# Fused linear attention and squared-ReLU MLP: where the attention's squares are kept, and how its slices are dealt out to the strips

## The chip, the cores and the metric

The kernel runs on one core of a Trainium2 chip. The metric is the device time of one execution in microseconds, from launch to end on that core. Lower is better. All arithmetic is fp32.

## The reference

Attention without a softmax feeds a two-layer MLP. `q`, `k` and `v` have 8 batches, 8 heads, 576 positions and a head size of 64.

```python
kv  = einsum('bhsd,bhse->bhde', k, v)          # 64 x 64 per head
out = einsum('bhsd,bhde->bhse', q, kv)
rms = sqrt(mean(out * out, axis=-1) + 1e-06)   # per head and position
x   = (out / rms * g_norm)                     # (8, 8, 576, 64)
x   = x.transpose(0, 2, 1, 3).reshape(4608, 512)
h   = x @ w_in                                 # 512 x 2048
r   = maximum(h, 0.0)
y   = (r * r) @ w_out                          # 2048 x 512
```

## The kernel before

The 4608 tokens are cut into 9 strips of 512, each of 4 tiles of 128 tokens. A strip has an up part (x times w_in, ReLU, square) and a down part (times w_out). The matrix products are Strassen-like: strip 0 is plain in its up part, strip 1 has one level there, and strips from 2 on (`DEEP_UP = 2`) have two levels. From strip 2 on the up part is 55 slots (`up_slot`), in each of which one or a few small products run as groups of four or eight 128 x 128 matmuls into a PSUM bank; the partial products that later sums need are copied out of PSUM as snapshots. In the profile these are the matmuls of L1109, the sums of L1121 on VectorE (DVE) or GpSimd (POOL), and the copies `snap` of L1126 on ScalarE (ACT). The ReLU and the square are L1059 and L1060. The down part is 14 steps of L921 matmuls, whose results are gathered in tiles `o_sb` and stored.

The attention that a strip needs is worked out while the strips before it run. It is one long list of steps, `slices`, and a step is a Python function that issues the instructions of one small piece of work:

- `transposed_query` (T) makes the transposed queries qT of a batch and a pair of heads,
- `key_value` (K) multiplies k and v to kv (L395) and copies it out (L398, L399),
- `query` multiplies qT and kv into PSUM, `x_ps` (L427), for up to two tiles of tokens, and squares the result on ACT (`sq`, L436); with extra arguments it also issues the `key_value` of a later batch,
- `mean_roots` reduces the squares on DVE (`ms`, L444) and takes the root,
- `normalized` divides (`x_n`, DVE, L495),
- `squares_x` transposes blocks of x_n on DVE into `x_q`, `send_x` stores x_q to DRAM (`x_d`, L571), and `fetch_x` reads it back transposed (`xT`, L577).

For strips 0 and 1 the shorter forms `query_means`, `roots_normalized` and `features` are used, in which the transposition is done by TensorE. `ready[s]` is the number of slices that have to be issued before strip s starts. Between the slots of strip s the function `attend` issues slices until the number due by then is reached, dealt out evenly. From strip 2 on:

```python
goal, begun = ready.get(s + 1, len(slices)), slice_at[0]
...
attend(begun + (goal - begun) * min(i + 1, 37) // 37)
```

So the order of the instructions on each engine is the order in which the Python functions are called; nothing reorders it afterwards. Each engine runs its instructions in that order and waits at an instruction whose inputs or whose output buffer aren't there yet. Nearly all DMAs are issued on SyncE's queue (SP), which waits in the same way. Each DMA also uses one of eight semaphores in turn, and so waits for the one eight before it.

Buffers come from pools that hand their buffers out in turn. Those that matter here are `xn` (3 buffers: x_n, x_q, and the squares sq), `c` (6 buffers: the snapshots and o_sb), `qkv` (2 each of q, k and v), and `stream` (4 buffers `w_blk`, the blocks of weights that are read from DRAM for each strip, issued by `stream`). The loads of q, k and v are issued by `load_next`, and in part one by one between the slots (`drip`; those of q are queued up by `drip_queries`). The remainder of 64 positions per batch is loaded by itself (`q_rest`, `k_rest`, `v_rest`).

Of the kernel before, what the change touches and what calls it, by code (L numbers as in the profile page):

```python
# [10 lines left out]
FP32 = mybir.dt.float32  # L11
# [9 lines left out]
def kernel(  # L21
# [47 lines left out]
    NT = 4  # L69
# [4 lines left out]
    DEEP_UP = 2  # L74
# [9 lines left out]
    xn_pool = ctx.enter_context(tc.tile_pool(name="xn", bufs=3))  # L84
# [86 lines left out]
    units = [(b, p) for b in range(B) for p in range(NP)]  # L171
    to_load = iter(units)

    owed = deque()

    def load_next(q_eng=nc.sync, names="kvq"):
        u = next(to_load, None)
        if u is not None:
            load(*u, q_eng, names)
            owed.extend([u] if "q" not in names else [])  # L180

    drips, rest_drips = deque(), deque()

# [4 lines left out]
                return f(*a)  # L188

    def drip_queries():  # L190
        if owed:
            u = owed.popleft()
            drips.extend((load, (*u, nc.sync, "q", (2 * h, 2 * h + 1))) for h in range(2))


# [216 lines left out]
    def products_x(ns):  # L412

        ps = apsum.tile([P, 2, 2, d_model // 2], FP32, name="x_ps", tag="x", bufs=1)
        for p in range(NP):
            for i, n in enumerate(ns):
                m, c = divmod(n, PAIR)
                for h in range(2):
                    half = slice(REST * h, REST * (h + 1))
                    if c == C:  # L420
                        q, b = qT["rest", m, p], 2 * m + h
                    else:
                        b, c_b = (2 * m, c) if c < C else (2 * m + 1, c - C - 1)
                        q = qT[b, p][:, c_b]
                    for r in range(2):
                        row = slice(D * r, D * (r + 1))
                        nc.tensor.matmul(  # L427
                            ps[half, r, i, ts(p, D)], lhsT=q[row, half], rhs=kvd[b, p][row, row], start=True, stop=True
                        )
        return ps  # L430

    def squared_parts(parts):
        sqs = []
        for ps in parts:
            sqs.append(xn_pool.tile(list(ps.shape), FP32, name="sq", tag="x_n"))
            nc.scalar.activation(sqs[-1], ps, AF.Square)  # L436
        return sqs

    def mean_of(sqs):
        ms = small.tile([P, 2, H], FP32, name="ms", tag="ms")[:, : len(sqs)]  # L440
        for i, sq in enumerate(sqs):
            if len(sq.shape) == 3:
                sq = sq.rearrange("p r e -> p (r e)")
            nc.vector.reduce_sum(out=ms[:, i], in_=by_head(sq), axis=AX.X)  # L444
        nc.vector.tensor_scalar(out=ms, in0=ms, scalar1=1.0 / D, scalar2=EPS, op0=ALU.mult, op1=ALU.add)
        return ms
# [17 lines left out]
    def query(ns, *keys):  # L464
        ps = products_x(ns)
        if keys:
            key_value(*keys)
        parts = [ps[:, :, i] for i in range(len(ns))]
        queried.append((parts, squared_parts(parts)))

    def query_means(ns):
        query(ns)
        parts, sqs = queried.pop()
        queried.append((parts, mean_of(sqs)))

    def roots_normalized(ns):
        parts, ms = queried.pop()
# [151 lines left out]
        slices += [(features, (n,)) for n in pair]  # L629
    ready[1] = len(slices)  # L630
    T, K, last = transposed_query, key_value, query_pairs(1)[2]
    slices += [(K, (2, 0, 1)), (T, (2, 0)), (query_means, (last,)), (T, (2, 1)), (roots_normalized, (last,))]
    slices += [(K, (2, 2, 3)), (features, (last[0],))]
    for b in range(2, B):
        fetch(1)
        slices += [(T, (b, p)) for p in (2, 3)]
        for pair in query_pairs(b):
            ahead = b + 1 < B and pair == query_pairs(b)[-1]
            slices.append((query, (pair, *((b + 1, 0, 1) if ahead else ()))))
            if ahead:  # L640
                slices += [(T, (b + 1, p)) for p in (0, 1)]
            slices.append((mean_roots, (pair,)))
            fetch(1)
            slices.append((normalized, (pair,)))
            fetch(1)
            slices += [(squares_x, (n,)) for n in pair]
            slices += [(send_x, (n,)) for n in pair]
            fetches.extend(pair)
            if ahead:
                fetch(1)  # L650
                slices.append((K, (b + 1, 2, 3)))
# [3 lines left out]
    def attend(n):  # L655
        while slice_at[0] < min(n, len(slices)):
            fn, a = slices[slice_at[0]]
            fn(*a)
            slice_at[0] += 1
# [499 lines left out]
    for s in range(N_STRIP):  # L1159
        attend(ready[s])  # L1160
        if s == DEEP_UP - 1:
            while queried:
                attend(slice_at[0] + 1)
            psums.close()
            fpsum = ctx.enter_context(tc.tile_pool(name="fpsum", bufs=5, space=bass.MemoryType.PSUM, reuse_waits="tile"))
            apsum = ctx.enter_context(tc.tile_pool(name="apsum", bufs=1, space=bass.MemoryType.PSUM, reuse_waits="tile"))
        if s >= DEEP_UP:
            steps = [(0.5, up_slot, (s, slot)) for slot in range(55)]
        elif s == 0:
            steps = [(2, up_first, (g, fh, i)) for g in range(NG) for fh in range(2) for i in range(2)]  # L1170
        else:
            steps = [(1, up, (s, g, p)) for g in range(NG) for p in ORDER]
        n_up = len(steps)
        if s < DEEP:

            steps += [(2, down, (s, p, i)) for p in (ORDER if s else (1, 2, 5, 6, 7, 3, 4)) for i in range(2)]
        else:
            steps += [(2, down_deep, (s, k, i)) for k in range(7) for i in range(2)]
        goal, begun = ready.get(s + 1, len(slices)), slice_at[0]
        total, done = sum(w for w, _, _ in steps), 0  # L1180
        for i, (w, fn, a) in enumerate(steps):
            if s == 0 and i < n_up:

                if 4 <= i < 11:
                    convert(5 + (3 * i + 2) // 4)
                if i in (4, 6, 8):
                    load_next()
                if i == 5:
                    load_rest(1, nc.sync)
                if i == 12:  # L1190
                    for b in range(2):
                        load_q_rest(b, nc.sync)
            elif s == 0 and i == n_up:
                convert(len(conversions))
                conv.close()

                stream_pool = ctx.enter_context(tc.tile_pool(name="stream", bufs=4, reuse_waits="tile"))
                sum_pool = ctx.enter_context(tc.tile_pool(name="sum", bufs=8, reuse_waits="tile"))
            if s == 0 and n_up <= i < n_up + 2:
                for g in range(2 * (i - n_up), 2 * (i - n_up) + 2):  # L1200
                    sum_g1(0, g)
            if s == 0 and n_up + 2 <= i < n_up + 4:
                for g in range(2 * (i - n_up) - 4, 2 * (i - n_up) - 2):
                    sum_g3(0, g)
            fn(*a)
            if s == 0 and i < 4:

                convert((3, 4, 5, 7)[i])
            done += w
            if s:  # L1210
                if i < n_up or i % 2:
                    drip(s == DEEP or i % 2 == 1)
                if s >= DEEP_UP:
                    attend(begun + (goal - begun) * min(i + 1, 37) // 37)
                else:
                    attend(begun + (goal - begun) * min(i + 1, n_up) // n_up)
                if s == DEEP and i == n_up - 3:
                    leaf_sums(s, 4)
                if s == 1 and i in range(3, 24, 3):
                    deep_sums_in((1, 6, 5, 4, 0, 2, 3)[i // 3 - 1])  # L1220
                if s == 1 and i in (n_up - 4, n_up - 2):
                    stream(2)
                continue
            if i == n_up + 1:
                stream()
            if i == n_up + 11:
                load_next()
            if i == n_up + 9:
                load_rest(2, nc.sync)
                load_q_rest(2, nc.sync)  # L1230
            if i - n_up in (7, 8, 9, 12):
                sums_in((7, 8, 9, 12).index(i - n_up))
            if i == n_up + 11:
                sums_x(1)
            n = i + 1 - (n_up - 6)
            pairs, m = divmod(max(n - 2 * NP, 0), 3)
            attend(min(ready[0] + min(max(n, 0), 2 * NP) + (n >= 2 * NP) + 4 * pairs + (0, 2, 2)[m], goal))
            if 11 <= i < n_up:

                convert(5 + (3 * i + 2) // 4)  # L1240
# [30 lines left out]
```

## Time and profile before

| | |
|---|---|
| median of 3 runs | 938.55 us (934.13 to 942.07) |
| profiled execution, whole | 936.43 us |
| its span in the profile | 934.6 us |
| mean granted TensorE clock | 0.983 |
| TensorE busy, matmuls / weight loads | 95% / 89% |
| DVE, ACT, POOL busy | 79%, 34%, 33% |
| DMA | 235.74 MB, mean 252 GB/s |
| chain that ended last | PE 74%, DVE 11%, DMA 9% |

The span is the time between the first and the last instruction of one execution under the profiler; 1.8 us of the execution lie outside it. PE is TensorE's matmuls and PEld its weight loads. A row of a timeline gives start, busy time, engine, line, operation, the tiles out and in, and in brackets the time that the engine was idle before it, with what released it. In a table of windows the columns after the window are its length, the busy time of each engine with the number of instructions, the granted clock as a share of full speed, the busy share of the DMA engines, and GB/s.

### The profile page before, as it was taken

Reading aid. Unit: us, or ns where it says so; the run is one execution under the profiler, and the core shown is the slowest. Engines: PE = TensorE matmul, PEld = TensorE weight load, DVE = VectorE, ACT = ScalarE, POOL = GpSimd, SP = SyncE. Lnnn points to the kernel's source line nnn. Section 1 sums busy time; section 2 is a strip of 40 time slices with the busy share of each in tenths; the row PEclk is TensorE's granted clock in tenths of the full one; section 3 lists DMA queues with packets and bytes.
Section 4 is the critical chain, followed back from the end, with each engine's and each line's share of the span. In section 5 each row is a group of like instructions: output and inputs, shape, how many; then the busy total and the mean of one; then the engine's idle time right before and its main releaser. Section 6 shows DMA issues by size and latency. Waiting matters only on the chain.

```text
span 934.6 us, 20804 instructions
## 1 busy us (share of the span) xinstructions
PE 890.0 (95%) x8246; PEld 830.9 (89%) x8246; DVE 738.8 (79%) x1258; ACT 318.2 (34%) x638; POOL 305.1 (33%) x315
## 2 busy tenths in 40 slices
PE   7999997999999999899998999699999999999998
PEld 6434786888989999899998999699999999999998
DVE  3899968778867996689777877589689967985886
ACT  4797350330024601280127112360155016302710
POOL 0000002810247505460455044330464147234700
PEclk7999999999999999999999999899999999999999
DMA  9699998879898786878776887878756866685385
GB/s 279 216 285 315 271 349 273 226 225 364 300 229 254 235 319 216 226 223 316 254 198 197 290 299 229 222 251 313 241 166 230 308 220 197 256 300 175 139 298 188
DMA packets 173810, 235.74 MB, mean 252 GB/s; under 512 B 85008, under 2 KB 138768, under 8 KB 165264
## 3 DMA queue, kind: packets, MB, share of 16 engines
q1 hardware_dynamic: 173392, 234.27, 77.8%
q8 instruction: 65, 1.06, 0.5%
q14 instruction: 33, 0.27, 0.1%
q10 hardware_dynamic: 320, 0.13, 0.1%
HBM read 197.66 MB, written 36.70 MB: 251 GB/s over the span
## 4 chain that ended last, share of the span: by engine, by line
PE 74%; DVE 11%; DMA 9%; issue 2%; SPq 2%; ACT 1%; DVEq 0%; ACTq 0%
PE ps_B L921 20%; PE ps_A L1109 17%; PE ps_A L921 15%; PE ps_B L1109 8%; PE ps_C L1109 4%; PE ps_A L700 3%; DMA x_d<-x_q 2%; PE x_ps L427 2%; PE kv_ps L395 1%; DVE w_c L251 1%; PE ps_B L700 1%; DMA w_blk<-w_in_deep 1%; DMA w_out<-w_in 1%; PE ps_C L700 1%; DMA k_rest<-in_k_dram 1%
## 5 line engine op out<-in xcount | busy, mean ns | idle before, releaser
L921 PE MATMUL ps_B<-w_blk,g_s 128*128 128x128 f32 x1024 | 125.9, 275 | 0.0
L921 PEld LDWEIGHTS ps_B<-w_blk,g_s 128*128 128x128 f32 x1024 | 120.1, 192 | 0.0
L1109 PE MATMUL ps_A<-x_l,w_in 128*128 128x128 f32 x784 | 107.0, 280 | 8.7 <-ACT snap L1126 5.8
L1109 PEld LDWEIGHTS ps_A<-x_l,w_in 128*128 128x128 f32 x784 | 97.6, 196 | 10.1 <-ACT snap L1126 5.3
L921 PE MATMUL ps_B<-w_blk,gt 128*128 128x128 f32 x768 | 97.6, 275 | 1.7 <-DMA w_blk<-w_out 1.3
L271 POOL TENSOR_TENSOR x_l<-xT 128x256 f32<-128x256 f32 x21 | 15.4, 735 | 248.9 <-PE ps_A L921 187.8
L921 PEld LDWEIGHTS ps_B<-w_blk,gt 128*128 128x128 f32 x768 | 91.4, 192 | 2.4 <-PE ps_A L700 1.3
L921 PE MATMUL ps_A<-w_blk,g_s 128*128 128x128 f32 x768 | 93.6, 275 | 0.0
L1121 POOL TENSOR_TENSOR snap<-snap,gt 128x512 f32<-128x512 f32 x35 | 45.9, 1310 | 138.1 <-ACT snap L1126 123.2
L921 PEld LDWEIGHTS ps_A<-w_blk,g_s 128*128 128x128 f32 x768 | 89.6, 192 | 0.0
L1126 ACT COPY snap<-ps_A 128x512 f32<-128x512 f32 x63 | 36.7, 582 | 116.7 <-PE ps_A L1109 97.9
L1059 ACT ACTIVATE gt<-gt 128x512 f32<-128x512 f32 x112 | 69.7, 622 | 15.8 <-DVE gt L1121 15.2
L921 PE MATMUL ps_A<-w_blk,gt 128*128 128x128 f32 x576 | 72.2, 275 | 0.0
L1060 ACT ACTIVATE gt<-gt 128x512 f32<-128x512 f32 x112 | 70.6, 631 | 3.6
L936 DVE TENSOR_TENSOR o_sb<-o_sb,ps_B 128x256 f32<-128x256 f32 (+1 forms) x128 | 49.5, 387 | 24.5 <-ACT o_sb L937 17.2
L921 PEld LDWEIGHTS ps_A<-w_blk,gt 128*128 128x128 f32 x576 | 68.2, 192 | 0.0
L1019 POOL TENSOR_TENSOR w_i<-w_in 128x512 f32<-128x512 f32 x7 | 9.8, 1399 | 159.3 <-PE kv_ps L395 156.4
L1121 POOL TENSOR_TENSOR gt<-gt,snap 128x512 f32<-128x512 f32 x42 | 52.4, 1277 | 26.6 <-DVE snap L1121 26.6
L271 DVE TENSOR_TENSOR gt<-gt 128x2048 f32<-128x2048 f32 (+1 forms) x29 | 59.7, 2063 | 0.0
L937 ACT COPY o_sb<-ps_A 128x128 f32<-128x128 f32 x24 | 6.4, 266 | 145.7 <-PE ps_A L921 145.7
L1121 DVE TENSOR_TENSOR gt<-ps_A,gt 128x512 f32<-128x512 f32 x49 | 33.0, 686 | 28.1 <-PE ps_A L1109 27.8
L1109 PE MATMUL ps_A<-x_l,w_blk 128*128 128x128 f32 x392 | 54.1, 283 | 0.0
(176 smaller groups left out, 1852.3 us busy)
## 6 DMA issues: line engine op xcount, KB each, us to landing
w_blk<-w_deep SPq DMA_DIRECT2D x56, 1024.0 KB, 6.5
w_blk<-w_out SPq DMA_DIRECT2D x56, 768.0 KB, 5.8
w_blk<-w_in_deep SPq DMA_DIRECT2D x49, 768.0 KB, 5.0
raw<-in_moe_w_in_dram SPq DMA_DIRECT2D x16, 512.0 KB, 6.2
raw<-in_moe_w_out_dram SPq DMA_DIRECT2D x16, 512.0 KB, 6.0
k<-in_k_dram SPq DMA_DIRECT2D x29, 256.0 KB, 5.2
v<-in_v_dram SPq DMA_DIRECT2D x29, 256.0 KB, 5.3
x_d<-x_q SPq DMA_DIRECT2D x27, 256.0 KB, 2.9
```

The source lines that it names most:

```text
L251: yield nc.vector.scalar_tensor_tensor(out=ci, in0=high, scalar=-(2**30), in1=ci, op0=ALU.bitwise_and, op1=ALU.bitwise_or)
L271: eng.tensor_tensor(out=out, in0=a, in1=b, op=ALU.subtract)
L427: nc.tensor.matmul(ps[half, r, i, ts(p, D)], lhsT=q[row, half], rhs=kvd[b, p][row, row], start=True, stop=True)
L700: nc.tensor.matmul(bank[BANK[p]][:, i, :], lhsT=lhsT(k), rhs=rhs(k), start=p in (1, 5, 2) and i == 0 and k == 0, stop=k == n - 1, skip_gro ...
L921: nc.tensor.matmul(chain[c][x][:, i, :], lhsT=a[:, f, :], rhs=w[:, f, :], start=x not in opened[c] and f == 0, stop=f == FQ // 2 - 1, skip ...
L936: add = lambda out, a, b: nc.vector.tensor_tensor(out=out, in0=a, in1=b, op=ALU.add)
L1019: nc.gpsimd.tensor_tensor(out=s1, in0=w_half(b, 0, 1), in1=w_half(b, 1, 1), op=ALU.add)
L1059: nc.scalar.activation(o, o, AF.Relu)
L1060: nc.scalar.activation(o, o, AF.Square)
L1109: nc.tensor.matmul(ps[:, i, :], lhsT=w, rhs=rhs, start=j in (1, 2, 5) and i == 0, stop=True, skip_group_check=True)
L1121: add = lambda eng, out, a, b: eng.tensor_tensor(out=out, in0=a, in1=b, op=ALU.add)
L1126: nc.scalar.copy(t, ps)
```

## The change

It has five parts.

1. `squared_parts` takes the pool as an argument. `query`, the form used from strip 2 on, puts its squares into the `c` pool; `query_means` and the opening keep them in `xn`.
2. From strip 2 on, the number of slices issued by the end of strip s is no longer just what strip s + 1 needs, but at least 24 for each strip since strip 2, as far as the first `fetch_x` of strip s + 2. They are dealt out over 38 instead of 37 slots. The slices issued in strips 2 to 7 were 25, 22, 21, 29, 21 and 14, and are now 25, 23, 24, 25, 22 and 13.
3. In strip 1, the second strip, the keys of batch 2 come later in the list: `K(2, 0, 1)` after the normalization of tile 8 instead of first, `K(2, 2, 3)` after `T(2, 2)`. Both `T(2, 2)` and `T(2, 3)` now stand in this list.
4. The q loads that `drip_queries` queues come from an iterator that begins at batch 2, pair 2, instead of from the list of units whose k and v were loaded without q. The sequence is the same, but q of (2, 2) is queued ahead of its k and v.
5. In strip 1, the two calls of `stream(2)` at the end of the up part come at steps 22 and 25 instead of 24 and 26.

The numbers of matmuls, copies and DMAs don't change. Line numbers in the changed file are one lower from `drip_queries` on up to `query`, and a little different after it.

```diff
--- before.py
+++ after.py
@@ -171,13 +171,12 @@
     units = [(b, p) for b in range(B) for p in range(NP)]
     to_load = iter(units)
 
-    owed = deque()
-
     def load_next(q_eng=nc.sync, names="kvq"):
         u = next(to_load, None)
         if u is not None:
             load(*u, q_eng, names)
-            owed.extend([u] if "q" not in names else [])
+
+    later_queries = iter(units[units.index((2, 2)) :])
 
     drips, rest_drips = deque(), deque()
 
@@ -188,8 +187,8 @@
                 return f(*a)
 
     def drip_queries():
-        if owed:
-            u = owed.popleft()
+        u = next(later_queries, None)
+        if u is not None:
             drips.extend((load, (*u, nc.sync, "q", (2 * h, 2 * h + 1))) for h in range(2))
 
 
@@ -429,10 +428,10 @@
                         )
         return ps
 
-    def squared_parts(parts):
+    def squared_parts(parts, pool=xn_pool, tag="x_n"):
         sqs = []
         for ps in parts:
-            sqs.append(xn_pool.tile(list(ps.shape), FP32, name="sq", tag="x_n"))
+            sqs.append(pool.tile(list(ps.shape), FP32, name="sq", tag=tag))
             nc.scalar.activation(sqs[-1], ps, AF.Square)
         return sqs
 
@@ -466,12 +465,12 @@
         if keys:
             key_value(*keys)
         parts = [ps[:, :, i] for i in range(len(ns))]
-        queried.append((parts, squared_parts(parts)))
+        queried.append((parts, squared_parts(parts, c_pool, "c")))
 
     def query_means(ns):
-        query(ns)
-        parts, sqs = queried.pop()
-        queried.append((parts, mean_of(sqs)))
+        ps = products_x(ns)
+        parts = [ps[:, :, i] for i in range(len(ns))]
+        queried.append((parts, mean_of(squared_parts(parts))))
 
     def roots_normalized(ns):
         parts, ms = queried.pop()
@@ -629,11 +628,12 @@
         slices += [(features, (n,)) for n in pair]
     ready[1] = len(slices)
     T, K, last = transposed_query, key_value, query_pairs(1)[2]
-    slices += [(K, (2, 0, 1)), (T, (2, 0)), (query_means, (last,)), (T, (2, 1)), (roots_normalized, (last,))]
-    slices += [(K, (2, 2, 3)), (features, (last[0],))]
+    slices += [(T, (2, 0)), (query_means, (last,)), (T, (2, 1)), (roots_normalized, (last,)), (K, (2, 0, 1))]
+    slices += [(features, (last[0],)), (T, (2, 2)), (K, (2, 2, 3)), (T, (2, 3))]
     for b in range(2, B):
         fetch(1)
-        slices += [(T, (b, p)) for p in (2, 3)]
+        if b > 2:
+            slices += [(T, (b, p)) for p in (2, 3)]
         for pair in query_pairs(b):
             ahead = b + 1 < B and pair == query_pairs(b)[-1]
             slices.append((query, (pair, *((b + 1, 0, 1) if ahead else ()))))
@@ -1177,6 +1177,10 @@
         else:
             steps += [(2, down_deep, (s, k, i)) for k in range(7) for i in range(2)]
         goal, begun = ready.get(s + 1, len(slices)), slice_at[0]
+        if s >= DEEP_UP:
+
+            ahead = [i for i, (fn, a) in enumerate(slices) if fn is fetch_x and a[0] // NT == s + 2]
+            goal = max(goal, min(ready[DEEP_UP] + 24 * (s - 1), *ahead[:1], len(slices)))
         total, done = sum(w for w, _, _ in steps), 0
         for i, (w, fn, a) in enumerate(steps):
             if s == 0 and i < n_up:
@@ -1211,14 +1215,14 @@
                 if i < n_up or i % 2:
                     drip(s == DEEP or i % 2 == 1)
                 if s >= DEEP_UP:
-                    attend(begun + (goal - begun) * min(i + 1, 37) // 37)
+                    attend(begun + (goal - begun) * min(i + 1, 38) // 38)
                 else:
                     attend(begun + (goal - begun) * min(i + 1, n_up) // n_up)
                 if s == DEEP and i == n_up - 3:
                     leaf_sums(s, 4)
                 if s == 1 and i in range(3, 24, 3):
                     deep_sums_in((1, 6, 5, 4, 0, 2, 3)[i // 3 - 1])
-                if s == 1 and i in (n_up - 4, n_up - 2):
+                if s == 1 and i in (n_up - 6, n_up - 3):
                     stream(2)
                 continue
             if i == n_up + 1:
```

## The prediction

> **What bounds the kernel now.** I first read the busy shares, then the chain of waits, then busy time by stage, the list of waits, and last the timelines around PE's gaps. From the page, the busy row and the chain's first row:
>
> ```profile
> PE 890.0 (95%) x8246; PEld 830.9 (89%) x8246; DVE 738.8 (79%) x1258; ACT 318.2 (34%) x638; POOL 305.1 (33%) x315
> PE 74%; DVE 11%; DMA 9%; issue 2%; SPq 2%; ACT 1%; DVEq 0%; ACTq 0%
> ```
>
> TensorE sets the end, and since no matmul is added or removed, only its gaps, and what they do to its clock, can pay. Strips count from 0. Stage by stage (each row runs from the same step of one strip's down part to that of the next: strips 2, 3, 4, 5, 6 and 8; columns: window, length, busy PE, PEld, DVE, ACT, POOL with counts, PEclk, DMA share, GB/s):
>
> ```profile
> 229.88:327.74 97.86, 94.72 (x1026) 93.43 (x1027) 79.65 (x130) 31.61 (x63) 46.82 (x47) 1.00 0.84 262
> 327.74:427.11 99.37, 95.34 (x995) 94.24 (x994) 77.50 (x132) 30.99 (x61) 38.17 (x40) 0.98 0.80 248
> 427.11:525.32 98.21, 94.04 (x955) 92.83 (x954) 76.36 (x127) 30.75 (x59) 37.76 (x40) 0.98 0.74 243
> 525.32:631.30 105.98, 98.63 (x1067) 97.40 (x1066) 80.65 (x132) 31.80 (x65) 38.12 (x40) 0.97 0.83 256
> 631.30:723.28 91.98, 91.70 (x955) 91.07 (x954) 76.75 (x127) 30.34 (x59) 38.30 (x40) 1.00 0.68 235
> 811.65:899.19 87.54, 87.54 (x786) 87.54 (x786) 66.51 (x102) 27.36 (x51) 38.11 (x40) 1.00 0.64 225
> ```
>
> Strip 8 has no attention: 87.54 is the floor. Strip 6 carries 21 slices of attention for 4.4 us more; strip 5 carries 29 and takes 18.4 more. The excess is gaps and clock. Five gaps on PE's timeline (last column: idle before, releaser):
>
> ```profile
> 157.93 0.69 PE L395 MATMUL kv_ps<-v,k 128*64 128x64 f32 x16 [3.34 <-DMA v<-in_v_dram]
> 393.71 1.54 PE L1109 MATMUL ps_B<-x_t,w_blk 128*128 128x128 f32 x8 [4.03 <-ACT snap L1126]
> 500.29 2.08 PE L1109 MATMUL ps_A<-x_l,w_in 128*128 128x128 f32 x8 [2.56 <-DVE gt L1121]
> 592.40 0.48 PE L395 MATMUL kv_ps<-v_rest,k_rest 128*64 128x64 f32 x4 [3.21 <-DMA v_rest<-in_v_dram]
> 602.71 2.08 PE L1109 MATMUL ps_A<-x_l,w_in 128*128 128x128 f32 x8 [4.14 <-ACT snap L1126]
> ```
>
> Two name ACT's snapshot copy; ACT's timeline (two sites) and DVE's at 499 show what stood ahead:
>
> ```profile
> 392.58 0.60 ACT L436 ACTIVATE sq<-x_ps 128x512 f32<-128x512 f32 x1 [5.47 <-DMA x_d<-x_q]
> 393.07 0.58 ACT L1126 COPY snap<-ps_B 128x512 f32<-128x512 f32 x1
> 601.59 0.60 ACT L436 ACTIVATE sq<-x_ps 128x512 f32<-128x512 f32 x1 [6.45 <-DMA x_d<-x_q]
> 498.95 0.69 DVE L495 TENSOR_TENSOR x_n<-x_ps,newton 128x512 f32<-128x512 f32 x1 [1.95 <-DMA x_d<-x_q]
> ```
>
> The square waited for one of the three xn buffers, held by an x_q whose store x_d had not landed; the snapshot behind it needed nothing. The list of waits has this twice (11.9 us), and two more squares behind DVE's reduction:
>
> ```profile
> ACT sq L436 <- DMA x_d<-x_q: 11.9, 2, 6.4
> ACT sq L436 <- DVE ms L444: 5.4, 2, 2.7
> ```
>
> A window of 3.4 us after a gap shows the granted clock (third column from the end), here after the gap of 2.03 us in strip 2 and the one of 4.03 in strip 3:
>
> ```profile
> 269.30:272.70 3.40, 3.40 (x85) 3.33 (x86) 1.57 (x3) 1.08 (x2) 0.00 (x0) 1.00 1.06 263
> 394.30:397.70 3.40, 3.40 (x19) 3.40 (x18) 3.37 (x7) 0.55 (x1) 3.24 (x3) 0.50 1.03 376
> ```
>
> **What the Trainium skill says.** TensorE: Matmul & The Clock Gate, "Part 1: The HAM clock gate": the clock falls to half after an idle window of about 3.4 us, free-running, and comes back after a busy one. The trace agrees on the length (0.50 for 3.4 us), but here 2.56 us of idle already did it; the 2.03 us at 269 did not. The price per long gap is 3.4 x 0.5 = 1.7 us. Same page, "Architectural detail": ACT and DVE are strict FIFO; the snapshot behind the square agrees. DMA: Bandwidth & Descriptors, "Anatomy of one DMA": a DMA's wait is served on the sequencer that issues it. On SP's timeline the fetches at L577 hold it from 573.44 to 579.64.
>
> **The change part by part.** No matmul, copy or DMA is added: each of the 36 squares still costs 597 ns, every x_d its 2.9 us. All effects are waits.
>
> *Squares into the c pool.* In strips 2 to 7 a square takes one of six c buffers, where a snapshot or an o_sb stood, and its waits in the built order are on snapshots and stores long past. The gaps at 393.71 and 602.71 go: 4.03 + 1.7 and 4.14 + 1.7 = 11.6. The squares behind DVE's reductions go too: by PE's timeline it lost 0.9 at 493.9 and 1.0 at 285.3 behind them. Sum -13.5. Cover: three live snapshots, two squares and one buffer under a POOL sum make six, so nothing is to spare in strip 5. ACT already waited 11.7 us in four places for o_sb stores, without PE noticing; if that moves ahead of a needed snapshot, one site costs what 393.71 did, 5.7. I take 0.
>
> *At most 24 slices per strip.* Counts for strips 2 to 7 go from 25, 22, 21, 29, 21, 14 to 25, 23, 24, 25, 22, 13. Strip 5's keys of batch 6 go from slot 19 to 16, and the sends and fetches that kept SP from their loads move to strip 4: loads issued 583.85 to 587.4 come about 8 us earlier, landing near 585 against a need at 589. The gap at 592.40 goes: 3.21 + 1.7 = 4.9. In strip 4 the sends stand four to five slots earlier; SP, late there (x_d issued at 494.33 after eight q_rest loads), gets to them before the stores. The gap at 500.29 goes: 2.56 + 1.7 = 4.3. Slices themselves only move: +3 in strip 4, -4 in strip 5.
>
> *Strip 1's order.* K(2,0,1) moves from step 0 to 4, some 7 us after PE's old arrival at 154.6 (157.93 less 3.34); its v landed at 157.8, so 3.34 + 1.7 = 5.0 goes. Late next: features of tile 8 needs DVE's x_n of about 165 to 166 (0 to 1.7 of stall), and K(2,2,3), at step 7, needs loads now issued behind q(2,3) at 166 to 169, landing 169 to 173 against PE at 169 to 170 (1.6 to 3.4, and perhaps another 1.7 of clock). Net from -5 to +2; I take -2.0.
>
> *Strip 1's streams.* Two blocks come two and one steps earlier; the fetch of tile 11 no longer holds the second pair. PE's three waits for w_blk at 216.11, 219.36 and 229.88 (0.91 + 0.34 + 0.43) go: -1.7.
>
> *q loads.* The same sequence with q(2,2) ahead of k and v(2,2): two DMAs past two on SP, 0. In strip 2, T(3,3) moves a slot and its 2.03 wait at 269.25 may grow by 0.65: +0.6.
>
> Sum: -13.5 - 4.9 - 4.3 - 2.0 - 1.7 + 0.6 = -25.8. Against this stands what comes late next. Small PE waits that no edit touches are 0.5 to 2.03 us, one or two per strip; some twenty slices in new slots should make one more in each of strips 2 to 6: 5 x 1.3 (the middle) = +6.5. That leaves -19.3. The profiled run took 936.43 (span 934.6 and 1.8 around it), giving 917.1; the three timed runs have a median of 938.55, 2.1 above it. I put the forecast at 918.0.
>
> **Rivals.**
> (a) *All of it goes*, nothing late next: -25.8, so 910.6 by the profiled run. For it: strips 6 to 8 show that a strip with 21 slices can run with 0.4 us of gaps. Against: DMA is busy 0.80 to 0.84 in the full strips, so loads land late.
> (b) *Only the squares pay*: strip 1 gives back what it saves, strip 4's and strip 5's loads stay late. -13.5 + 3 = -10.5, 926 to 928. For it: SP's lateness in strip 4 comes from q_rest loads that stay.
> (c) *The wait changes its name*: with squares free of xn, DVE's x_n and SP's queue wait instead, and PE stands as long: within 1%, 930 to 938. For it: the gap at 500.29 is just that kind. Against: x_n stands several slots later than the square in strips 3 and 5.
> (d) *Slower*: squares hold up the snapshots in the c pool. A square takes a buffer that a snapshot would have had, and the next snapshot waits for an o_sb store or a POOL sum (1.3 us each) at the strip's head, with PE behind it. One such site is 5.7. The squares' 13.5 then isn't won, the other parts bring 12.3 less 3.5 returned, -8.8; it decides from two sites among the fifteen queries, and three make +8.3: 945. For it: four ACT waits on these stores exist already. Against: those had no PE gap after them.
>
> **How the numbers follow.** Forecast (most go) 0.45, (a) 0.15, (b) 0.18, (c) 0.12, (d) 0.10. A measurement here tells from no change about 1%, 929.2 and 947.9. Three quarters of (b) lies below: faster 0.45 + 0.15 + 0.14 = 0.74; same 0.04 + 0.12 = 0.16; slower 0.10. The range, 906 to 933, takes in (a) at its bottom (opening at its best, -5 instead of -2, less the run-to-run spread), all of (b) and half of (c); it leaves out (d), half of (c) and a little of (a), 0.2.
>
> **What would show it.** Right: no ACT square waiting for x_d; no snapshot-released gap of PE over 2 us in strips 3 and 5; the stage of strip 5 near 95 us, of strip 3 near 93.5, of strip 4 near 93; PEclk 1.00 in them; kv_ps not waiting in strip 5; a smaller wait at strip 1's K(2,2,3). Wrong: x_n on DVE waiting over 2 us for x_d with PE behind, snapshots waiting for o_sb stores with PE behind, or new stalls for v or q in strips 1 and 4 of over 2.5 us, each with a dip of the clock.

## The result and the profile after

The changed kernel takes 935.68 us (median of 20 runs), the kernel before 939.42 in the same measurement. The ratio is 0.9972 with a 95% interval of 0.9949 to 0.9995: a gain of 0.3%, where 2% was forecast. The profiled execution has a span of 933.4 us against 934.6.

The page of the changed kernel, the busy row and the chain's first row:

```profile
PE 886.8 (95%) x8246; PEld 827.4 (89%) x8246; DVE 731.7 (78%) x1258; ACT 318.3 (34%) x638; POOL 305.5 (33%) x315
PE 70%; DVE 14%; DMA 7%; SPq 4%; issue 3%; ACT 1%; DVEq 0%; ACTq 0%
```

SP's own queue was 2% of the chain before and is 4% now. The table of windows, cut at the same matmuls as before (strips 2, 3, 4, 5, 6 and 8; window, length, busy times, PEclk, DMA share, GB/s):

```profile
230.21:328.72 98.51, 96.09 (x1028) 94.83 (x1026) 79.58 (x132) 31.42 (x63) 46.73 (x47) 0.98 0.82 262
328.72:427.92 99.20, 93.95 (x995) 92.61 (x994) 77.74 (x133) 30.86 (x61) 38.13 (x40) 1.00 0.80 250
427.92:520.20 92.28, 92.10 (x955) 91.21 (x953) 75.97 (x128) 30.56 (x59) 38.28 (x40) 1.00 0.82 264
520.20:628.79 108.59, 97.91 (x1066) 96.34 (x1065) 77.08 (x130) 32.13 (x65) 38.21 (x40) 0.97 0.81 244
628.79:721.97 93.18, 92.34 (x955) 91.35 (x953) 78.27 (x133) 30.28 (x59) 38.10 (x40) 1.00 0.67 232
810.33:897.88 87.55, 87.55 (x786) 87.55 (x785) 66.50 (x102) 27.34 (x51) 38.05 (x40) 1.00 0.65 226
```

Only strip 4 is as forecast (98.21 to 92.28), and its 98.21 was itself high: a kernel below that changes nothing in strip 4 takes 94.9 there. Strip 3 stands where it stood (99.37, now 99.20), and strip 5, from which 11 us were to go, is 2.6 longer. What became of the gaps is seen on ACT's timeline, at the two snapshot copies that used to stand behind a square:

```profile
395.26 0.58 ACT L1126 COPY snap<-ps_A 128x512 f32<-128x512 f32 x1
603.09 0.57 ACT L1126 COPY snap<-ps_A 128x512 f32<-128x512 f32 x1
```

No idle time stands before them: the squares no longer hold ACT up, and the list of waits has no square waiting for x_d. But PE has new gaps (its timeline, last column the idle time and releaser):

```profile
172.59 0.69 PE L394 MATMUL kv_ps<-v,k 128*64 128x64 f32 x16 [1.80 <-DMA v<-in_v_dram]
175.30 1.12 PE L394 MATMUL kv_ps<-v,k 128*64 128x64 f32 x16 [1.91 <-DMA v<-in_v_dram]
416.12 1.13 PE L921 MATMUL ps_B<-w_blk,gt 128*128 128x128 f32 x8 [3.67 <-DMA w_blk<-w_deep]
586.39 0.34 PE L394 MATMUL kv_ps<-v_rest,k_rest 128*64 128x64 f32 x4 [2.32 <-DMA v_rest<-in_v_dram]
615.15 2.05 PE L921 MATMUL ps_B<-w_blk,gt 128*128 128x128 f32 x8 [7.46 <-DMA w_blk<-w_deep]
```

The third and the fifth are new in kind: at the head of the down parts of strips 3 and 5, PE waits for the first block `w_deep`. The kernel before had no wait there: its matmul on that block (PE's timeline) started without idle time.

```profile
619.53 1.06 PE L921 MATMUL ps_B<-w_blk,gt 128*128 128x128 f32 x8
```

SP's timeline shows why. In the kernel before:

```profile
406.66 0.38 SPq L805 DMA_DIRECT2D w_blk<-w_deep  x1
612.24 1.24 SPq L121 DMA_DIRECT2D q<-in_q_dram  x2
613.57 0.56 SPq L805 DMA_DIRECT2D w_blk<-w_deep  x1
```

and in the changed one:

```profile
410.81 0.38 SPq L805 DMA_DIRECT2D w_blk<-w_deep  x1
600.18 7.81 SPq L121 DMA_DIRECT2D q<-in_q_dram  x8
608.04 2.04 SPq L576 DMA_DIRECT2D xT<-x_d  x4
610.18 0.38 SPq L805 DMA_DIRECT2D w_blk<-w_deep  x1
```

PE came to the down part of strip 5 at 615.95 before and comes at 603.95 now, 12.0 us earlier. SP comes to the block 3.4 us earlier. In strip 3 PE is 3.1 us earlier (411.76 to 408.71) and SP 4.2 later.

The old gaps had to do with the same queue. In the kernel before, DVE had written the two x_q of strip 5 by 588.6, but SP issued their stores only at 599.50, after k, v, q and q_rest loads (DVE's timeline, then SP's):

```profile
587.92 0.69 DVE L562 STREAM_TRANSPOSE x_q<-x_n 128x512 f32<-128x512 f32 x1
599.50 0.85 SPq L571 DMA_DIRECT2D x_d<-x_q  x2
```

So PE's old gaps in the up part and the new one at the down part's head are two waits for the same queue: before, PE stood behind the x_d store that SP was late with, and by the time it then came to the down part, SP had also issued w_deep.

### The profile page after: what moved, and what is told of

It is laid out like the page before. It is cut to its first block, busy times and chain, and to the rows that moved or that the text cites. A ratio compares the mean times of both kernels' runs of the same rounds, so it can differ in the third digit from the quotient of the medians.

```text
span 933.4 us, 20822 instructions
## 1 busy us (share of the span) xinstructions
PE 886.8 (95%) x8246; PEld 827.4 (89%) x8246; DVE 731.7 (78%) x1258; ACT 318.3 (34%) x638; POOL 305.5 (33%) x315
## 4 chain that ended last, share of the span: by engine, by line
PE 70%; DVE 14%; DMA 7%; SPq 4%; issue 3%; ACT 1%; DVEq 0%; ACTq 0%
PE ps_B L921 21%; PE ps_A L921 16%; PE ps_A L1109 15%; PE ps_B L1109 7%; PE ps_C L1109 4%; SPq L121 2%; PE x_ps L426 2%; DVE gt L1121 2%; PE ps_A L700 2%; DMA v<-in_v_dram 1%; PE kv_ps L394 1%; SPq L576 1%; DVE w_c L250 1%; DMA w_out<-w_in 1%; DVE w_t L270 1%
## 5 line engine op out<-in xcount | busy, mean ns | idle before, releaser
L921 PEld LDWEIGHTS ps_B<-w_blk,gt 128*128 128x128 f32 x768 | 92.3, 193 | 12.9 <-issue 11.5
L1109 PEld LDWEIGHTS ps_A<-x_l,w_in 128*128 128x128 f32 x784 | 96.8, 194 | 1.3 <-ACT snap L1126 0.7
L921 PE MATMUL ps_A<-w_blk,g_s 128*128 128x128 f32 x768 | 93.6, 275 | 0.0
L1059 ACT ACTIVATE gt<-gt 128x512 f32<-128x512 f32 x112 | 69.7, 622 | 25.9 <-DVE gt L1121 25.8
```

The source lines that it names most:

```text
L921: nc.tensor.matmul(chain[c][x][:, i, :], lhsT=a[:, f, :], rhs=w[:, f, :], start=x not in opened[c] and f == 0, stop=f == FQ // 2 - 1, skip ...
L1059: nc.scalar.activation(o, o, AF.Relu)
L1109: nc.tensor.matmul(ps[:, i, :], lhsT=w, rhs=rhs, start=j in (1, 2, 5) and i == 0, stop=True, skip_group_check=True)
```

## The experiments

Theory A: SP's queue of loads sets the time in strips 3 and 5, the first `w_deep` block is its next deadline, and with a wait ahead of it removed, PE stands there instead. The rivals: the squares are the whole gain and the other parts eat it (B), or the DMA engines, not the order, are the limit (C).

To read the experiments side by side, here is the time between the same matmuls of one strip and the next, from PE's timeline of each profiled execution (us), and the ratio of the times to those of the kernel before:

| kernel | strip 2 | 3 | 4 | 5 | 6 | ratio (95%) |
|---|---|---|---|---|---|---|
| before | 97.8 | 99.4 | 98.2 | 106.0 | 92.0 | 1 |
| changed | 98.5 | 99.2 | 92.3 | 108.6 | 93.2 | 0.9972 (0.9949 to 0.9995) |
| squares back in xn | 98.3 | 105.6 | 92.9 | 110.3 | 93.2 | 1.001 (0.999 to 1.0031) |
| squares alone | 96.8 | 96.4 | 94.7 | 109.2 | 92.0 | 0.9999 (0.997 to 1.0027) |
| changed, q held | 97.1 | 96.0 | 93.4 | 103.7 | 94.5 | 0.9883 (0.984 to 0.9926) |
| before, q held | 97.7 | 101.0 | 95.5 | 104.1 | 92.0 | 0.9995 (0.9973 to 1.0016) |
| squares alone, q held | 96.9 | 94.5 | 94.4 | 101.9 | 92.0 | 0.9891 (0.9844 to 0.9938) |
| strip 1's parts alone | 97.7 | 100.6 | 94.9 | 106.0 | 92.0 | 1.0015 (0.9991 to 1.004) |
| changed, w_deep on ACT | 99.0 | 95.5 | 93.0 | 106.1 | 93.2 | 0.9927 (0.9903 to 0.9951) |
| q held, w_deep on ACT | 98.8 | 95.3 | 92.3 | 104.5 | 93.3 | 0.9871 (0.9827 to 0.9915) |
| q, k, v held | 97.2 | 96.8 | 94.0 | 103.8 | 93.5 | 0.9937 (0.9913 to 0.9961) |
| q held longer | 97.1 | 100.1 | 94.8 | 98.8 | 94.2 | 0.9887 (0.9846 to 0.9929) |
| q, k, v held longer | 97.1 | 95.3 | 95.7 | 100.5 | 93.6 | 0.99 (0.9848 to 0.9952) |

Strips 7 and 8 are the same in all (88.4 and 87.5, once 89.1). What lies before strip 2 differs by up to 6 us from one profiled execution to another (the down part of strip 1 begins between 213.9 and 219.8), mostly in waits at 15 to 100 us that no kernel here changes. A strip's row is thus sharper than one profiled span, but it is one execution too: strip 4 takes 98.2 in the kernel before and 94.9 with strip 1's parts alone, which change nothing in it, so differences of 3 us between two rows can be chance.

### The changed kernel with the squares back in xn

```diff
-        queried.append((parts, squared_parts(parts, c_pool, "c")))
+        queried.append((parts, squared_parts(parts)))
```

> The changed kernel with part 1 undone: the squares of the later queries stand in the xn pool again. Theory A (what was won on ACT is lost again at the head of the down parts, where PE waits for the first w_deep block, because SP's queue of loads is as late as PE was): the ACT gaps of strips 3 and 5 come back (4.0 and 4.1 us, 1.7 of clock each), and the w_deep waits of 3.7 and 7.5 us shrink by about as much; 934 to 938 us, much the same as the changed kernel. Theory B (the squares are the whole gain of the change, the other parts cost about as much): the gaps come back in full, the w_deep waits stay, 945 to 948.

Measured: 936.95 us, ratio 1.001. ACT's and PE's timelines:

```profile
397.43 0.60 ACT L435 ACTIVATE sq<-x_ps 128x512 f32<-128x512 f32 x1 [9.69 <-DMA x_d<-x_q]
398.55 1.22 PE L1109 MATMUL ps_B<-x_t,w_blk 128*128 128x128 f32 x4 [8.25 <-ACT snap L1126]
606.68 1.22 PE L1109 MATMUL ps_A<-x_l,w_in 128*128 128x128 f32 x4 [9.35 <-ACT snap L1126]
```

The gaps come back, twice as long as in the kernel before, and neither w_deep wait is left. Theory B's 945 to 948 did not come. The time is that of theory A, though the gaps are 8.25 and 9.35 where it had 4.0 and 4.1: in this execution the strips lose more (105.6 and 110.3) than the median shows; its profiled run, 942.61 us, lies 5.7 above the median. Without the new place for the squares, the other parts of the change bring nothing.

### The kernel before with the squares alone

The diff is part 1 of the change.

> The kernel before with part 1 alone: squares in the c pool, nothing else changed. Theory A: the snapshot gaps go in strips 2 to 5 (-13 with the clock), but w_deep is issued no earlier than before (near 406.7 and 613.6), so PE waits for it at the down part: about 2 us in strip 3 and 5 to 6 in strip 5, with 1.7 of clock; 934 to 937. Theory B (as forecast, the squares alone pay in full): 925 to 927.

Measured: 935.99 us, ratio 0.9999. PE's timeline:

```profile
414.54 1.13 PE L921 MATMUL ps_B<-w_blk,gt 128*128 128x128 f32 x8 [1.62 <-DMA w_blk<-w_deep]
615.88 1.41 PE L921 MATMUL ps_B<-w_blk,gt 128*128 128x128 f32 x5 [5.22 <-DMA w_blk<-w_deep]
```

Theory A's numbers, about 2 and 5 to 6. What strips 2, 3 and 4 win (1.0, 3.0, 3.5) strip 5 spends in part (3.2). Of the 4.3 us left, this execution lost 3.2 ahead of strip 2, and the runs show no gain (interval 0.997 to 1.0027).

### The changed kernel with the q loads held back

```diff
-                if i < n_up or i % 2:
+                if (i < n_up or i % 2) and not (s >= DEEP_UP and 26 <= i < 49):
                     drip(s == DEEP or i % 2 == 1)
```

> The changed kernel with the queued q loads held back between slots 26 and 48 of strips 2 to 8, so that eight of them no longer stand ahead of the first w_deep block on SP in strips 3 and 5. Same DMAs, other order. Theory A: w_deep is issued 5 to 8 us earlier, its waits of 3.7 and 7.5 us and the 1.7 of clock after the second go; 922 to 926. Theory C (not the order on SP but the DMA engines' throughput is the bound, so something else lands late by as much): 933 to 937, with waits of the same sum at other blocks.

Measured: 923.55 us, ratio 0.9883. SP's timeline, then PE's:

```profile
594.37 3.46 SPq L576 DMA_DIRECT2D xT<-x_d  x4
598.33 0.34 SPq L805 DMA_DIRECT2D w_blk<-w_deep  x1
605.23 1.02 PE L921 MATMUL ps_B<-w_blk,gt 128*128 128x128 f32 x7 [2.23 <-DMA w_blk<-w_deep]
```

The block is issued at 598.33 instead of 610.18, the wait in strip 5 is 2.23 instead of 7.46, and in strip 3 there is none at the first block. No load was left out; the hold also keeps back the q_rest loads that stand in the same list. So it was the order on SP that turned the gain into a new wait, and with it repaired, the change is worth about 1.2% (0.7 to 1.6%).

### The kernel before with the same loads held back

The same edit on the kernel before.

> The kernel before with the same q loads held back. Theory A: before, PE came to w_deep just as it landed and waited for nothing there, so there is nothing to win: 937 to 941, the ACT gaps of strips 3 and 5 unchanged. Theory D (these loads cost time wherever they stand, and the change has nothing to do with it): 926 to 930.

Measured: 935.04 us, ratio 0.9995: nothing, as theory A had it (its 937 to 941 was too high, since the kernel before ran at 936.15 in this measurement). Its ACT gaps are there (PE's timeline), of other sizes than before:

```profile
397.63 1.23 PE L1109 MATMUL ps_B<-x_t,w_blk 128*128 128x128 f32 x4 [5.04 <-ACT snap L1126]
603.92 0.82 PE L1109 MATMUL ps_A<-x_l,w_in 128*128 128x128 f32 x5 [1.70 <-ACT snap L1126]
```

The squares alone give nothing, the held loads alone give nothing. Together:

### The squares alone, with the loads held back

> The kernel before with part 1 (squares in the c pool) and the q loads held back between slots 26 and 48; no slice budget, old strip 1. Theory A (the squares and the room on SP pay only together, and the other parts are worth what their own gaps measure): the w_deep waits of the squares alone (1.8 and 5.4 us) shrink below 2.5 in sum, the gaps at v_rest in strip 5 (3.0 and 1.7 of clock) and at x_n in strip 4 (about 1.8) stay; 926 to 930. Theory E (the slice budget is what makes the held kernel fast): 933 to 937.

Measured: 927.58 us, ratio 0.9891, which the held changed kernel's 0.9883 can't be told from. No w_deep wait stands at the head of strips 3 and 5; PE waits 2.57 us for v_rest at 585.42 and 1.27 at 494.20, about as expected, without the clock dip that I had added to the first. The slice budget and strip 1's order are thus not what makes the held kernel fast. In the table the budget wins in strip 4 (94.4 without, 93.4 with it; 94.7 and 92.3 where nothing is held, no more than chance can make) and gives it back in strip 6, which is 92.0 in every kernel without it and 93.2 to 94.5 in every kernel with it.

### Strip 1's parts alone

Parts 3, 4 and 5 of the change on the kernel before.

> The kernel before with parts 3, 4 and 5 alone (strip 1's order of keys, q loads, earlier streams). My forecast had -2.0 for the order and -1.7 for the streams. Theory A': the first wait for v (3.3 us) is exchanged for two of about 2 us each at the two later keys, so the order gives 0; the streams give at most 1; 935 to 938 against 936 to 939 of the kernel before. Rival (the forecast): 3 to 4 us faster. The trace tells these apart better than the time.

Measured: 936.84 us, ratio 1.0015. PE's timeline:

```profile
174.32 0.69 PE L394 MATMUL kv_ps<-v,k 128*64 128x64 f32 x16 [2.48 <-DMA v<-in_v_dram]
176.65 1.12 PE L394 MATMUL kv_ps<-v,k 128*64 128x64 f32 x16 [1.53 <-DMA v<-in_v_dram]
```

The one wait for v of 3.34 us became two, 4.0 together, both at `K(2, 2, 3)`. The streams did what they were to: at the first w_blk of the down part PE waits 0.28 instead of 0.91, and not at all at the next. That is too small for the runs to show.

### The first w_deep block from ACT's queue

```diff
-                nc.sync.dma_start(out=t, in_=w_deep[B_OUT[p]])
+                (nc.scalar if p == 4 and u[0] >= DEEP_UP else nc.sync).dma_start(out=t, in_=w_deep[B_OUT[p]])
```

> The changed kernel with the first w_deep block of each strip from 2 on issued from ACT's queue instead of SP's: seven DMAs of 129 or so, the same bytes, and no other order. Theory A (it is the place behind sixteen loads and fetches on SP that makes it late): it is issued when PE frees its buffer, about 598 instead of 610 in strip 5 and 402 instead of 411 in strip 3, both waits go; 922 to 927, unless ACT, which waits with it, delays snapshots by more than 1 us. Theory C (the 16 DMA engines are full, so the block or the loads beside it land as late as before): 932 to 937.

Measured: 929.41 us, ratio 0.9927, between the two theories. ACT's timeline, then PE's:

```profile
597.60 0.33 ACTq L805 DMA_DIRECT2D w_blk<-w_deep  x1
618.57 1.19 PE L921 MATMUL ps_A<-w_blk,gt 128*128 128x128 f32 x4 [4.21 <-DMA w_blk<-w_out]
```

The block leaves at 597.60, and both w_deep waits at the down parts' heads are gone. But the next block, w_out, is still on SP behind the q loads and the fetch, is issued at 613.43, and PE waits 4.21 us for it. One step further along the same queue, the same thing happened again: theory A, with one more deadline than I had written into the number.

### Both cures

> Both cures on the changed kernel: q loads held back, and the first w_deep block from ACT's queue. The held kernel still waits 2.4 us for w_deep in strip 5. Theory A: that one goes too, 920 to 923. If the two cures take away the same wait and ACT pays for the issue: 923 to 926.

Measured: 924.34 us, ratio 0.9871. The second of the two cases: the wait of 2.23 us in strip 5 is gone, and one of 2.70 at 616.33, for a later w_deep, has come.

### k and v held back too

```diff
-                load_next(names="kv")
+                if b in (5, 7) and p < 2:
+                    u = next(to_load, None)
+                    if u is not None:
+                        drips.append((load, (*u, nc.sync, "kv")))
+                else:
+                    load_next(names="kv")
```

with a loop at the head of `key_value` that issues what is still queued for its own batch and pair.

> The held kernel (the changed one with q loads held back between slots 26 and 48) with the two pairs of k and v loads that follow the first keys of batches 5 and 7 put into the same queue, so that they too come after the first w_deep block in strips 3 and 5. Theory A: SP reaches w_deep some 3 us earlier in strip 5, and its last wait there (2.4 us) goes; nothing is left to win in strip 3, where the held kernel has none; 920 to 923. If the 1 MB of k and v then stands ahead of the second w_deep or w_out block, the wait moves there: 923 to 926.

Measured: 929.29 us, ratio 0.9937, worse than both cases that I gave. PE's timeline:

```profile
622.40 0.80 PE L928 MATMUL ps_B<-w_blk,gt 128*128 128x128 f32 x5 [3.77 <-DMA w_blk<-w_out]
```

The first w_deep is in time, but six q loads, now pushed behind k and v, take SP from 607.45 to 614.63, and the w_out behind them leaves at 617.15. The wait moved on once more.

### The longer hold

```diff
-                if (i < n_up or i % 2) and not (s >= DEEP_UP and 26 <= i < 49):
+                if (i < n_up or i % 2) and not (s >= DEEP_UP and 26 <= i < n_up + 3):
```

> As the held kernel, but the q loads stay back until the third step of the down part is over, so that they stand ahead of none of its first five w blocks. Theory A: in strip 5 the first w_deep wait (2.2 us) stays, since k, v and the fetches ahead of it are the same, and the small waits for later blocks (0.5 and 0.9 us) go: 921 to 923. If the loads then come too late for the next strip's queries, a new wait at T or K in strip 4 or 6 makes it 926 or more.

> As the kernel that holds back k and v too, with the same longer hold. Theory A: there the wait moved to a w_out block (3.8 us and the clock after it) because six q loads stood ahead of it; with these out of the way no block of the down part is late in strips 3 and 5: 917 to 921, the best of all. Theory C (the engines cannot move the bytes in time in whatever order): the wait appears at yet another place, 925 to 930.

Measured: 925.12 (ratio 0.9887) with q alone, 927.44 (ratio 0.99) with k and v too. With q alone the wait for w_deep in strip 5 shrinks to 0.89, and the strip is the shortest of all (98.8), but in strip 3, where the first held kernel had none, PE now waits 2.21 us for w_deep, with a clock dip after it (100.1; PE's timeline with q alone):

```profile
410.54 1.25 PE L921 MATMUL ps_B<-w_blk,gt 128*128 128x128 f32 x8 [2.21 <-DMA w_blk<-w_deep]
```

With k and v too, no block of the down parts of strips 3 and 5 is late any more, so the w blocks can be moved in time. The time is nevertheless not below the first held kernel's: PE stands 2.76 us for v_rest in strip 5 and twice for sums of DVE in strip 4 (1.57 and 1.23). My 917 to 921 was a miss, and 927.44 lies in theory C's range. That theory's first form, that a changed order on SP wins nothing, fell with the first held kernel; how much the DMA engines themselves still cost here, these runs don't show. Of the five kernels with squares in c and a ratio between 0.987 and 0.990 none can be told from another. Each of them beats the kernel before, and all but the last in the table, whose interval touches that of the changed kernel, beat the changed one too.

## Why the prediction was wrong

**The step that failed is the term for what comes late next: +6.5, "5 x 1.3 (the middle)".** I sized it by the small waits left over in the kernel before. In the two profiled executions the parts, which were to give 25.8, gave 1.2, so the term had to be some 24.6. By the stages, strip 5 falls short of its forecast by 13.3, strip 3 by 5.6, what lies ahead of strip 2 by 4.0, and strips 6 and 2 by 1.2 and 1.1; strip 4 beats it by 0.7. The largest pieces are the two waits for w_deep, 3.67 and 7.46 us, and the clock dip that began during the second. Three windows of the changed kernel, after the gaps of strips 2, 3 and 5 (PEclk third from the end):

```profile
270.87:274.28 3.41, 3.41 (x18) 3.41 (x17) 0.82 (x2) 0.92 (x2) 0.00 (x0) 0.50 0.83 273
416.10:419.50 3.40, 3.38 (x30) 3.40 (x31) 1.32 (x3) 0.60 (x1) 0.00 (x0) 1.00 0.97 405
615.15:619.03 3.88, 3.88 (x18) 3.88 (x19) 0.09 (x1) 0.00 (x0) 0.00 (x0) 0.50 0.97 395
```

So 3.67 + 7.46 + 1.9 (3.88 us at half clock) = 13.0 came back in two places, twice the term. It could have been read before: SP issued w_deep at 613.57 and PE needed it at 619.53, 6.0 us later, while the page's median for its landing is 6.5. The slack at that block was next to nothing, so a PE that is 12 us earlier can keep only what SP is earlier.

Step by step:

- *Squares, -13.5.* The mechanism was right: no square waits for x_d, and no snapshot waits behind one. The worth was wrong for this kernel: by itself the edit gives 0.9999. With room on SP the same edit takes the ratio from 0.9995 to 0.9891, some 10 us, so the size of the two gaps was near and what stood behind them was missing. The fear of rival (d), snapshots held up in the c pool, did not come about.
- *Slice budget, -4.9 and -4.3.* The gap at x_n in strip 4 went with the strip's others (98.21 to 92.28, forecast -5.2 with the squares' part). That is in part luck: I priced the gap of 2.56 us and its clock dip from one execution, and with q held the kernel before shows 1.35 us there and no dip, with strip 1's parts alone none over 0.8 us. The gap at v_rest in strip 5 did not go: 3.21 became 2.32, since the load landed 6.0 us earlier but PE reached it 5.1 us earlier too. Only its clock dip went (PEclk 1.00 after it). And strip 6 pays 1.2, which I had at nothing.
- *Strip 1's order, -2.0.* It gave about 0: the wait of 3.34 at `K(2, 0, 1)` went, and 1.80 and 1.91 at `K(2, 2, 3)` and 0.50 at the features of tile 8 came, with one clock dip before and one after. The 3.7 us at `K(2, 2, 3)` and the dip after it lie at the upper end of what I had named (3.4 and 1.7); the middle was too hopeful.
- *Streams, -1.7.* About half: 0.93 of the 1.68 remains in the changed kernel, 0.28 in strip 1's parts alone.
- *qT_rest in strip 2, +0.6.* The wait stayed as it was (1.86 us on PE's timeline in both kernels, where I had written 2.03), yet this time the clock fell after it, to 0.50 for 3.4 us from 270.87 on, which costs 1.7.
- *Rivals.* (c), the wait changes its name, is what happened, with "SP's queue" as the new name; I gave it 0.12 and had looked for it at x_n and not at the weights of the down part. (a) and (b) both assumed that a gap on ACT can be won for itself.

What stays open: why SP in strip 3 of the changed kernel comes to w_deep 4.2 us later than before. It is late by 1.0 at the start of the strip, by 1.8 when the q_rest loads begin (385.36 to 387.19), by 2.9 when the fetches begin (401.77 to 404.68); no run takes that apart. With the squares alone it comes 3.0 later (409.69), of which 2.2 stand already at the start of the strip. Nor do the runs part the worth of the slice budget from nothing once the loads are held.

## What to carry to other kernels

When an in-order queue is late, the engine that computes may wait for it at its first late item only, and what stands behind that item then looks as if it were in time, as w_deep did here. Before pricing the removal of such a wait, follow the same queue to the next transfers that the engine needs and write down each one's slack, need less landing; the gain ends where the first slack does. A cure for the wait and a cure for the queue's order can each be worth nothing alone (0.9999 and 0.9995 here) and about 1% together (0.9891, interval 0.9844 to 0.9938). A price read from one execution, of a gap or of a clock dip, should be checked against a second one.

## What the hardware did that I had not expected

The clock after a gap doesn't follow from the gap's length alone. Idle of 3.67 us at 416 and of 2.32 us at 586 left it at 1.00, while 2.56 us in the kernel before brought it to 0.50, and a wait of 1.86 us at the same place in strip 2 was followed by 1.00 in one kernel and by 0.50 in the other. The Trainium skill (TensorE: Matmul & The Clock Gate, "Part 1: The HAM clock gate") has the window free-running, so that the phase decides. The traces agree: within an execution the clock changes only at times a whole number of windows of 3.41 us apart. In the kernel before it falls at 394.32, 500.14 and 592.30, and the distances 105.82 and 92.16 are 31 and 27 times 3.413. Cut at this grid, the gaps fall into place (two windows of the kernel before, then three of the changed one; after the length comes PE's busy time, PEclk is third from the end):

```profile
496.72:500.14 3.42, 1.01 (x10) 0.82 (x8) 1.47 (x3) 1.78 (x4) 0.24 (x1) 1.00 1.00 383
500.14:503.55 3.41, 3.26 (x15) 3.26 (x16) 1.99 (x4) 3.21 (x6) 1.44 (x2) 0.50 0.47 136
410.81:414.23 3.42, 1.64 (x15) 1.45 (x13) 2.78 (x4) 2.33 (x4) 3.30 (x2) 1.00 0.86 253
414.23:417.64 3.41, 1.52 (x13) 1.55 (x14) 0.00 (x0) 0.65 (x2) 0.00 (x0) 1.00 1.01 418
417.64:421.05 3.41, 3.41 (x33) 3.41 (x32) 1.89 (x3) 1.40 (x3) 0.00 (x0) 1.00 0.51 216
```

Nearly all of the gap of 2.56 us lay in one window, which had 2.41 us of idle, and the clock was at half in the next. The gap of 3.67 us was split over two windows, with 1.78 and 1.89 us of idle, and the clock stayed up. Over the 13 traces, from 100 us on, all 30 windows at full clock in which PE's matmuls were idle for 1.95 us or more were followed by half clock, none of the 43 with 1.0 to 1.76 us was, and of the 17 in between 7 were. Here the page and the measurement differ: the page asks for an idle window of about 3.4 us, and in these traces idle in somewhat more than half of one was enough. A fixed price of 1.7 us for every gap over 2.3, as I used, is too sharp.
